# The first batch of a retention-and-Fourier kernel rebuilt: order of loads, sums on TensorE, an order of units written out by hand

## The chip, the core and the metric

One NeuronCore of a Trainium2 chip runs the kernel. The metric is the device time of one execution in microseconds; lower is better. A profile is one execution, recorded instruction by instruction; its span goes from the first to the last instruction, and the device time is a little longer than the span.

## What is computed

Inputs are q, k, v of shape (4 batches, 8 heads, 768 positions, 64), and two weights of 512 x 2048 and 2048 x 512. The first half is a linear recurrence with decay, the second a Fourier mixing and a feed-forward net:

```python
for t in range(S):                                    # S = 768
    state = gamma * state + k[:, :, t] (x) v[:, :, t] # outer product, per batch and head
    y[:, :, t] = scale * q[:, :, t] @ state
x = y as (batch, 768, 512)
X = fft(fft(x, axis=1), axis=2)
u = x + real(X)
un = (u - mean(u)) / sqrt(var(u) + 1e-6)              # over the 512 columns
out = u + relu(un @ w_ch1) @ w_ch2
```

## The kernel before

**The recurrence** is done in six chunks of 128 positions, two heads (a pair) at a time, four pairs per batch. q and k of a pair are cast to f16 (`q0_unit`, `k0_unit`; k is scaled by its decay, giving `kd`), transposed on TensorE (`t0_unit`, tile `tq`) and copied out of PSUM (`te_unit`: `qT`, `kT`). Scores inside a chunk (`am_unit`, tile `wkA`) are masked on VectorE (`ae_unit`, tile `atm`, four instructions per pair). Products of k and v per chunk (`kv0_unit`, tile `wkK`) go through a scan over the chunks (`sc_unit`, tile `s`). The output of a pair collects both parts in PSUM (`yi_unit`: masked scores times v; `yx_unit`: q times the states, tile `wkY`) and is scaled into `x` (`x0_unit`).

**The Fourier part** is two products with cosine and sine tables. Rows 0 to 383 and 384 to 767 of x are added and subtracted (`fold_s`, tile `xab`), then the two sides of the model axis (`fold_d`, tile `eo`), all on VectorE. Four products with the tables over the positions follow (`s1_unit`, tile `ps`, cast to `g`), then products with the tables over the model axis (`s2_unit`, tile `pq`), whose two halves are combined on VectorE, with ScalarE's copy `qn`, into `u`. The tables themselves are computed in the kernel: angles on VectorE (`trig_dve`), sines on ScalarE (`t_act`, `csn_unit`). In the first batch the first three blocks of 128 rows take a shorter way: `px_unit` puts x into PSUM by matmuls with half-identity matrices, and the mean comes from sums over x (`xmean_unit`).

**The feed-forward part** transposes `un` (`unT_unit`) and runs 16 blocks of the first product (`h0_unit` for the first half of batch 0, 128 rows at a time, tile `psh`; `h_unit` elsewhere), evicted with a relu by ScalarE or VectorE as `ACT_ROWS` says, and the second product (`ch_unit`, tile `psc`), whose result is scaled, added to u and stored.

**Order.** Batch 0's first part runs alone: `first_units` lists its units by hand, and `pin` makes every engine keep that order. `filler` matmuls with a zero operand stand in between. Everything behind is emitted from streams that have a start and an end in turns (`DM0`, `TS0`, `DA0`, `LD0` and so on), and is merged by those numbers: the feed-forward part of one batch beside the recurrence and the Fourier part of the next.

**Transfers.** Twelve loads of 384 KB bring batch 0: nine on SP's queue (L185), v of pairs 1 to 3 on ScalarE's queue. Eight DMAs of 512 KB bring the weights, cast to f16 on the way, issued by GpSimd (`w1_unit`, `w2_unit`) among its casts. The loads of batch 1 (L165) wait for the seventh weight DMA and for the last matmul of the second 128 rows of `h0_unit`:

```python
for x in (w_dma[after].ins, lb[0]["mm"].ins):         # after = 6
    tc.add_manual_dep(dma.ins, x.name, ...)
```

Of the kernel before, what the change touches and what calls it, by code (L numbers as in the profile page):

```python
# [18 lines left out]
P = 128  # L19
# [10 lines left out]
PAIR_ORDER = [0, 1, 3, 2]  # L30
ON_ACT = {'q': (0, 1, 0), 'kv': (1, 1, 1), 'g': (0, 1, 1), 'gr': (0, 0, 0)}
FB = 1
DM0, DM1 = (0.120, 0.208, 0.265, 0.344), (0.004, 0.137, 0.232, 0.341)
TS0 = (0.249, 0.368, 0.406, 0.410, 0.479, 0.544, 0.680, 0.685)
TS1 = (-0.040, -0.020, 0.048, 0.585)
DA0, DA1 = (0.068, 0.080, 0.173, 0.203, 0.315, 0.321), (0.063, 0.067, 0.063, 0.158, 0.168, 0.189)
LD0, LD1 = (0.172, 0.226), (-0.370, 0.140)
HT0 = (0.655, 0.675, 0.673, 0.628)
NPE = 2
ACT_ROWS = ((2, 5, 6, 7, 8, 9, 10, 14), (0, 3, 6, 7, 9, 10, 11, 12, 14, 15), (2, 4, 5, 6, 7, 8, 10, 14))  # L40
# [3 lines left out]
def kernel(  # L44
# [42 lines left out]
    cd16 = const.tile([P, 2, 257], f16, tag="cd16", padded_shape=[P, 2, 260])  # L87
    sd16 = const.tile([P, 2, 257], f16, tag="sd16", padded_shape=[P, 2, 260])
# [5 lines left out]
    gk5 = const.tile([P, NHP, D, NCH - 1], f32, tag="gk5")  # L94
# [85 lines left out]
    def first_load(name, i, eng):  # L180
        def run():
            h0 = 2 * PAIR_ORDER[i]
            t = in_of[name, 0, i] = inp.tile([P, 2, NCH, D], f32, tag="in32", name=f"{name}32")
            rows = "h (p c) d -> p h c d" if name == "q" else "h (c p) d -> p h c d"
            eng.dma_start(t, srcs[name][0, h0:h0 + 2].rearrange(rows, p=P))  # L185
        return run

    for i in range(4):
        for name in "qkv":
            if name != "v" or i == 0:  # L190
                first_load(name, i, nc.sync)()
# [34 lines left out]
    first_load("v", 1, nc.scalar)()  # L226
# [13 lines left out]
    def gk_unit(hp):  # L240
        def run():
            nc.scalar.copy(gk5[:, hp, :, 1:], gk2[:, hp:hp + 1].unsqueeze(1).to_broadcast(
                [P, D, NCH - 2]))
        return run
# [36 lines left out]
    def parity_consts():  # L281
        nc.vector.tensor_scalar(out=m2, in0=icol[:, 0:1], scalar1=0.5, scalar2=-0.25,
                                op0=ALU.mult, op1=ALU.add)
        nc.vector.tensor_scalar(out=m2, in0=m2, scalar1=MAGIC, scalar2=-MAGIC,
                                op0=ALU.add, op1=ALU.add)
        nc.vector.scalar_tensor_tensor(out=odd, in0=m2, scalar=-2.0, in1=icol[:, 0:1],
                                       op0=ALU.mult, op1=ALU.add)
        nc.vector.tensor_copy(pmask[:, 1:4:2], odd.to_broadcast([P, 2]))
        nc.vector.tensor_scalar(out=pmask[:, 0:4:2], in0=pmask[:, 1:4:2], scalar1=-1.0,
                                scalar2=1.0, op0=ALU.mult, op1=ALU.add)  # L290
        nc.vector.tensor_scalar(out=sgn, in0=odd, scalar1=-2.0, scalar2=1.0,
                                op0=ALU.mult, op1=ALU.add)

    def trig_dve(idx, n, w, col, coln):
        r = rs[2 * idx][:, 0:w]
        ra = rs[2 * idx + 1][:, 0:w]

        def run():
            nc.vector.tensor_scalar(out=ra, in0=kf[:, 0:w], scalar1=coln, scalar2=MAGIC,
                                    op0=ALU.mult, op1=ALU.add)  # L300
            nc.vector.tensor_scalar(out=ra, in0=ra, scalar1=-MAGIC, scalar2=float(n),
                                    op0=ALU.add, op1=ALU.mult)
            nc.vector.scalar_tensor_tensor(out=r, in0=kf[:, 0:w], scalar=col, in1=ra,
                                           op0=ALU.mult, op1=ALU.subtract)
        return run

    def ts_dve(c):
        return trig_dve(c, S, KN, icol[:, c:c + 1], icoln[:, c:c + 1])

    def csn_unit(c):  # L310
        def run():
            nc.scalar.activation(csn[:, c, :], rs[2 * c + 1][:, 0:384], AF.Sin, bias=hpi,
                                 scale=-float(2.0 * np.pi / S))
        return run

    def td_dve(c):
        return trig_dve(3 + c, DM, 257, icol[:, 3 + c:4 + c], icoln[:, 3 + c:4 + c])

    def t_act(idx, part):
# [5 lines left out]
        def run():  # L325
            if part == 0:
                nc.scalar.activation(ra, r, AF.Abs, bias=0.0, scale=1.0)
            elif idx < 3:
                src = (ra, r)[part - 1].rearrange("p (i t) -> p t i", t=2)
                dst = (csp, ssp)[part - 1]  # L330
                nc.scalar.activation(dst[:, :, idx, :], src, AF.Sin,
                                     bias=hpi if part == 1 else 0.0,
                                     scale=-sc if part == 1 else sc)
            else:
                src, dst = (ra, r)[part - 1], (cd16, sd16)[part - 1]
                nc.scalar.activation(dst[:, idx - 3, :], src, AF.Sin,
# [16 lines left out]
    hid, nhid = xts[1][:, 0, 0, 0:P], xts[1][:, 0, 1, 0:P]  # L353

# [5 lines left out]

    def half_ids():
        nc.gpsimd.tensor_scalar(out=hid, in0=ident16, scalar1=0.5, scalar2=1.0, op0=ALU.mult,
                                op1=ALU.mult)
        nc.gpsimd.tensor_scalar(out=nhid, in0=ident16, scalar1=-0.5, scalar2=1.0, op0=ALU.mult,
                                op1=ALU.mult)
# [47 lines left out]
    def k0_unit(i):  # L413
        def run():
            h0 = 2 * PAIR_ORDER[i]
            k32 = in_of.pop(("k", 0, i))
            kd = kd_of[0, i] = kp.tile([P, NCH, 2, D], f16, tag="kd16", name="kd16")
            nc.gpsimd.tensor_scalar(out=kd[:, :, 0, :], in0=k32[:, 0], scalar1=gkd[:, h0:h0 + 1],
                                    scalar2=1.0, op0=ALU.mult, op1=ALU.mult)
            if i < 3:  # L420
                nc.gpsimd.tensor_scalar(out=kd[:, :, 1, :], in0=k32[:, 1],
                                        scalar1=gkd[:, h0 + 1:h0 + 2], scalar2=1.0,
                                        op0=ALU.mult, op1=ALU.mult)
            else:
                nc.scalar.activation(kd[:, :, 1, :], k32[:, 1], AF.Copy, bias=0.0,
                                     scale=gkd[:, h0 + 1:h0 + 2])
        return run

    def v0_unit(i):
        def run():  # L430
            v32 = in_of.pop(("v", 0, i)).rearrange("p h c d -> p c h d")
            v16 = v16_of[0, i] = vp.tile([P, NCH, 2, D], f16, tag="v16", name="v16")
            n = NCH if i < 3 else 3
            last_cast[0, i] = nc.gpsimd.tensor_scalar(
                out=v16[:, 0:n], in0=v32[:, 0:n], scalar1=1.0, scalar2=1.0, op0=ALU.mult,
                op1=ALU.mult)
            if n < NCH:
                nc.vector.tensor_copy(v16[:, n:], v32[:, n:])
# [14 lines left out]
    def te_unit(i, part):  # L453
        def run():
            st = at[0, i]
            tq = st["tq", part]
            if part == 0:
                nc.scalar.copy(st["qT"].rearrange("p c t -> p (c t)").rearrange(
                    "p (t c) -> p t c", c=NCH), tq.rearrange("p c t -> p t c"))
            else:  # L460
                nc.scalar.copy(st["kT"], tq)
# [17 lines left out]
    def ae_unit(i, half, h2):  # L479
        def run():  # L480
# [3 lines left out]
                scalar=float(gam[2 * PAIR_ORDER[i] + h2] ** (-P)),  # L484
# [16 lines left out]
    def sc_unit(i):  # L501
        def run():
# [5 lines left out]
                data0=gk5[:, PAIR_ORDER[i]].rearrange("p e c -> p (e c)"),  # L508
# [3 lines left out]
    def yi_unit(i, h2):  # L512
        def run():
            st = at[0, i]
            first = i < 3
            if first:
                st["y", h2] = ps_y.tile([P, NCH, D], f32, tag="y", name="wkY",
                                        padded_shape=[P, 8, D])
            y, atm, v16 = st["y", h2], st["atm"], v16_of[0, i]
            for c in range(NCH):  # L520
                nc.tensor.matmul(y[:, c, :], atm[:, c, h2, :], v16[:, c, h2, :],
                                 start=first and c == 0, stop=not first and c == NCH - 1,
                                 skip_group_check=True)
        return run

    def yx_unit(i):
        def run():
            st = at[0, i]
            first = i == 3
# [663 lines left out]
```

## Time and profile before

| | us |
|---|---|
| median of 3 runs | 249.33 |
| lowest and highest | 247.75, 250.26 |
| span of the profiled execution | 246.5 |

Busy time of the engines and the span in 40 slices of 6.2 us (each digit is the busy share in tenths):

```profile
PE 233.7 (95%) x2024; PEld 144.1 (58%) x2024; DVE 177.0 (72%) x430; ACT 123.8 (50%) x276; POOL 81.0 (33%) x146
...
PE   6498899999999998999999999999999999999995
...
DVE  8689976897797878997886738897895657424112
ACT  2998769577775444662247424741248317202500
POOL 6657700465610047791000555670002305000000
DMA  8999999599999567999999657786200241221012
```

PE is TensorE, PEld its weight loads, DVE VectorE, ACT ScalarE, POOL GpSimd, SP the engine that issues most DMAs; a q behind a name is that engine's queue of DMA issues. "idle before" names what an engine waited for last.

### The profile page before, as it was taken

How to read it: one execution, taken by the hardware profiler on the slowest of the kernel's cores; microseconds unless marked ns; L12 is line 12 of the kernel's file. 1: busy time of each engine (PE TensorE's matmuls, PEld its weight loads, DVE VectorE, ACT ScalarE, POOL GpSimd, SP SyncE). 2: the span in 40 equal slices, each digit the busy share in tenths (PEclk: the TensorE clock that was granted, in tenths of full speed). 3: DMA queues.
4: the chain of work that ended last, by engine and by line, in shares of the span. 5: the costliest groups of instructions: out<-in, count | busy, mean ns of one | idle time of the engine just before them, and what ended most of it. 6: DMA issues, size and time to landing. Idle time of an engine off the chain costs nothing.

```text
span 246.5 us, 5306 instructions
## 1 busy us (share of the span) xinstructions
PE 233.7 (95%) x2024; PEld 144.1 (58%) x2024; DVE 177.0 (72%) x430; ACT 123.8 (50%) x276; POOL 81.0 (33%) x146
## 2 busy tenths in 40 slices
PE   6498899999999998999999999999999999999995
PEld 2165568956676655665567546565667455445543
DVE  8689976897797878997886738897895657424112
ACT  2998769577775444662247424741248317202500
POOL 6657700465610047791000555670002305000000
DMA  8999999599999567999999657786200241221012
GB/s 174 258 257 139 185 202 198 129 257 239 276 237 223 100 143 165 200 183 131 258 276 214 123 116 215 141 116 142 86 1 0 45 149 23 47 85 43 0 45 85
DMA packets 99209, 36.39 MB, mean 148 GB/s; under 512 B 89840, under 2 KB 96240, under 8 KB 99184
## 3 DMA queue, kind: packets, MB, share of 16 engines
q1 hardware_dynamic: 90304, 30.68, 58.9%
q0 software_dynamic: 4224, 4.19, 10.6%
q10 hardware_dynamic: 4656, 1.18, 2.9%
q8 instruction: 16, 0.26, 0.5%
q14 instruction: 9, 0.07, 0.1%
HBM read 27.26 MB, written 6.29 MB: 136 GB/s over the span
## 4 chain that ended last, share of the span: by engine, by line
PE 67%; DMA 10%; DVE 7%; ACT 5%; SPq 4%; POOL 4%; issue 2%; POOLq 0%; ACTq 0%; DVEq 0%
PE psc L990 30%; PE psh L947 24%; DMA k<-in_k_dram 8%; SPq L185 4%; PE ps L747 3%; PE wkA L611 3%; DMA q<-in_q_dram 2%; PE wkY L665 2%; PE wkY L661 1%; POOL u L881 1%; PE pq L844 1%; DVE bst L900 1%; POOL u L883 1%; DVE u L851 1%; ACT un L896 1%
## 5 line engine op out<-in xcount | busy, mean ns | idle before, releaser
L990 PE MATMUL psc<-w,ht 128*128 128x512 f16 (+2 forms) x400 | 89.3, 370 | 0.0
L947 PE MATMUL psh<-unT,w 128*128 128x384 f16 x448 | 81.6, 326 | 0.4 <-ACT ht L951 0.2
L990 PEld LDWEIGHTS <-ht 128*128 128x128 f16 x400 | 37.6, 98 | 36.4 <-issue 0.2
L947 PEld LDWEIGHTS <-w 128*128 128x128 f16 x448 | 42.3, 98 | 24.7 <-issue 1.4
L951 ACT ACTIVATE ht<-psh 128x384 f16<-128x384 f32 x64 | 30.9, 490 | 41.6 <-PE psh L947 41.1
L881 POOL TENSOR_TENSOR u<-u,x 128x256 f32<-128x256 f32 x21 | 13.4, 636 | 100.2 <-DVE u L851 89.7
L994 DVE SCALAR_TENSOR_TENSOR ob<-psc,stats,u 128x512 f32<-128x512 f32 (+2 forms) x25 | 18.1, 726 | 26.1 <-PE psc L990 26.0
L953 DVE TENSOR_SCALAR ht<-psh 128x384 f16<-128x384 f32 x48 | 26.2, 549 | 7.7 <-PE psh L947 7.3
L614 DVE TENSOR_TENSOR atm<-wkA,maskp 128x512 f16<-128x512 f32 x36 | 23.8, 683 | 1.6 <-PE wkA L611 1.6
L902 ACT ACTIVATE un<-u,stats 128x512 f16<-128x512 f32 x21 | 15.2, 722 | 16.5 <-DVE stats L901 12.3
L900 DVE BATCH_NORM_STATS2 bst<-u 128x6 f32<-128x512 f32 x21 | 14.6, 695 | 7.8 <-POOL u L883 7.6
L640 DVE SCALAR_TENSOR_TENSOR s<-s,gk,wkK 128x128 f16<-128x128 f16 x48 | 16.4, 342 | 3.5 <-ACT s L636 2.5
L673 ACT ACTIVATE x<-wkY,gexp 128x384 f16<-128x384 f32 x24 | 12.8, 581 | 8.2 <-PE wkY L665 8.2
L394 POOL TENSOR_SCALAR kd<-k,gexp 128x384 f16<-128x384 f32 x24 | 13.9, 588 | 3.6 <-DMA k<-in_k_dram 3.6
L151 PE MATMUL wps<-ht 128*128 128x512 f16 x40 | 13.0, 429 | 2.2 <-POOL ht L212 2.2
L883 POOL TENSOR_TENSOR u<-u,x 128x256 f32<-128x256 f32 x21 | 13.3, 636 | 3.0 <-DVE stats L901 2.4
L611 PE MATMUL wkA<-qTz,kT 128*128 128x256 f16 x72 | 13.4, 272 | 0.1
L846 ACT COPY qn<-pq 128x128 f32<-128x128 f32 x18 | 4.9, 273 | 13.5 <-PE pq L844 13.5
L964 PE MATMUL psh<-unT,w 128*128 128x128 f16 x192 | 11.5, 219 | 0.1
L964 PEld LDWEIGHTS <-w 128*128 128x128 f16 x192 | 11.0, 98 | 0.7 <-issue 0.5
L851 DVE SCALAR_TENSOR_TENSOR u<-pq,g,qn 128x256 f32<-128x256 f32 x18 | 8.5, 473 | 3.3 <-PE psh L947 2.5
L399 POOL TENSOR_SCALAR v<-v 128x768 f16<-128x768 f32 x12 | 10.0, 832 | 1.4 <-DMA v<-in_v_dram 1.3
(164 smaller groups left out, 315.0 us busy)
## 6 DMA issues: line engine op xcount, KB each, us to landing
q<-in_q_dram SPq DMA_DIRECT2D x16, 384.0 KB, 6.3
k<-in_k_dram SPq DMA_DIRECT2D x16, 384.0 KB, 5.9
out_dram<-ob SPq DMA_DIRECT2D x23, 256.0 KB, 2.7
v<-in_v_dram SPq DMA_DIRECT2D x13, 384.0 KB, 5.8
w<-in_moe_w_ch_dram POOLq DMA_DIRECT2D x8, 512.0 KB, 11.0
v<-in_v_dram ACTq DMA_DIRECT2D x3, 384.0 KB, 9.7
unT<-un SPq DMA_TRANSPOSE x15, 2.4
out_dram<-ob SPq DMA_DIRECT2D x1, 192.0 KB, 1.9
```

Of the source, the lines that this page charges most:

```text
L611: mm = nc.tensor.matmul(wk[:, c2], st["kT"][:, c, :], st["qT"][:, :, c, :], start=True, stop=True)
L614: nc.vector.tensor_tensor(out=st["atm"][:, 2 * part:2 * part + 2], in0=wk, in1=maskp[:, PAIR_ORDER[i]].unsqueeze(1).to_broadcast([P, 2, 2, ...
L640: nc.vector.scalar_tensor_tensor(out=s16[:, c], in0=s16[:, c - 1], scalar=gk2[:, hp:hp + 1], in1=wk[:, c - c0], op0=ALU.mult, op1=ALU.add)
L881: nc.gpsimd.tensor_tensor(out=u[:, kb, 0:256], in0=u[:, kb, 0:256], in1=x[:, kb, 0, 1:257], op=ALU.add)
L883: nc.gpsimd.tensor_tensor(out=u[:, kb, 256:512], in0=u[:, kb, 256:512], in1=x[:, kb, 1, 257:1:-1], op=ALU.add)
L900: nc.vector.bn_stats(bst, u[:, kb, :])
L947: nc.tensor.matmul(psh, w116[:, cb, fb * P:(fb + 1) * P], unT[:, cb, rt * 384:(rt + 1) * 384], start=(cb == 0), stop=(cb == 3))
L951: nc.scalar.activation(ht16[:, fb, :], psh, AF.Relu, bias=0.0, scale=-1.0)
L953: nc.vector.tensor_scalar(out=ht16[:, fb, :], in0=psh, scalar1=-1.0, scalar2=0.0, op0=ALU.mult, op1=ALU.max)
L964: mm = nc.tensor.matmul(psh[:, f], w116[:, cb, fb * P:(fb + 1) * P], unT[:, cb, kb * P:(kb + 1) * P], start=(cb == 0), stop=(cb == 3))
L990: nc.tensor.matmul(psc[:, c0:c1], ht16[:, fb, rb3 * P:(rb3 + 1) * P], w216[:, fb, c0:c1], start=(fb == 0), stop=(fb == NFB - 1))
L994: nc.vector.scalar_tensor_tensor(out=ob[:, c0:c1], in0=psc[:, c0:c1], scalar=lb[b]["st"][:, rb, 3:4], in1=lb[b]["u"][:, rb, c0:c1], op0=AL ...
```

## The change

Nothing is left out of the computation. In batch 0's first part:

- All twelve loads go on SP's queue, in a new order of pairs and with v of the last two pairs at the end.
- `first_units` becomes a string of unit names, `FIRST`, with the engine behind an @ where there is a choice (v VectorE, a ScalarE, g GpSimd). Casts of k and v, copies of the transposes, evictions of x and two table steps are split or moved by it.
- `fold_d` falls away: the sum over the two sides of the model axis is made by TensorE, which adds the products of both sides in PSUM (`s1b_unit`, with a negated sine table `ssn`). Each pair's columns of x are folded as soon as they are there (`fold_p`).
- The tables over the model axis are mirrored to 512 columns (`flip_unit`), so that a whole row of u stands in one PSUM tile; x is added by identity matmuls (`sa_unit`), and one instruction moves u out (`ua_unit`). The first block's centered rows are taken straight from PSUM (`n0_unit`); the others use the statistics.
- The position table `csn` is copied from the other tables on GpSimd, not computed by ScalarE.

Behind it the turns of the streams and `ACT_ROWS` take other numbers.

```diff
+ORD0 = [1, 0, 3, 2]
+LOADS0 = [("q", 0), ("k", 0), ("v", 0), ("q", 1), ("k", 1), ("v", 1), ("q", 2), ("k", 2),
+          ("q", 3), ("k", 3), ("v", 2), ("v", 3)]
+FIRST = """
+tsa2@g tsa0@v ts0 q0 ta00 ta01 ta02 xe1 k01@a k00@a ts2 tsa4@v fill6 t00 e00@a tsa3@g fill5 t01
...
+yi10 ta22 ae101 ae111 yi11 ta30 yx1 am20 gk2 k31@g fs0 s010 v21@g am21 t30 x11@v k30@a
+ae201 gk3 e30@a ae211 x10@v t31 e31@a ae210 fill4 am30 am31 ta41 w0 ae200 v32@g v22@v ae300 kv2
+sc2 s110 fl2@g yi21 yi20 ae310 ta31 fs1 yx2 v31@a x20@a w1 w2 s100 s000 ae311 ae301 kv3 yi31
+x21@a fs2 s001 sc3 s101 yi30 yx3 fl3@g x31@v ge00@a ge10@a x30@a fs3 gr2 xs0@a xs3@v csn w3
+sa00 sa10 sa11 g0 s011 s111 ge01@a xs1@v ge11@v gr0 sa20 sa02 sa01 sa03 g1 xs2@a mean sa22
+nh0@v g2 nh1@a sa12 pt0 gr3 sa13 ua0 sa21 pe0@a ua1 sa23 pt1 pe1@a gr1 bn1 ua2 w4 w5 w6 w7 bn2
+n1 n2
+"""
-DM0, DM1 = (0.120, 0.208, 0.265, 0.344), (0.004, 0.137, 0.232, 0.341)
-TS0 = (0.249, 0.368, 0.406, 0.410, 0.479, 0.544, 0.680, 0.685)
+DM0, DM1 = (0.101, 0.194, 0.248, 0.334), (-0.003, 0.131, 0.160, 0.383)
+TS0 = (0.282, 0.345, 0.387, 0.439, 0.487, 0.518, 0.675, 0.686)
...
-ACT_ROWS = ((2, 5, 6, 7, 8, 9, 10, 14), (0, 3, 6, 7, 9, 10, 11, 12, 14, 15), (2, 4, 5, 6, 7, 8, 10, 14))
+ACT_ROWS = ((5, 6, 7, 8, 9, 10, 13, 14), (0, 3, 6, 9, 12, 14, 15), (2, 4, 5, 7, 8, 10, 14))
...
-    for i in range(4):
-        for name in "qkv":
-            if name != "v" or i == 0:
-                first_load(name, i, nc.sync)()
+    for name, i in LOADS0:
+        first_load(name, i, nc.sync)()
...
+    def csn_unit():
+        for c in range(3):
+            nc.gpsimd.tensor_copy(csn[:, c].rearrange("p (i t) -> p t i", t=2),
+                                  csp[:, 0:2, c, 0:192])
...
+    def flip_unit(n, eng):
+        e = {"v": nc.vector, "g": nc.gpsimd}[eng]
+        out, in0, m = ((ssn, ssp, -1.0), (cd16[:, :, 257:512], cd16[:, :, 255:0:-1], 1.0),
+                       (sd16[:, :, 257:512], sd16[:, :, 255:0:-1], -1.0))[n - 2]
+
+        def run():
+            e.tensor_scalar(out=out, in0=in0, scalar1=m, scalar2=1.0, op0=ALU.mult,
+                            op1=ALU.mult)
+        return run
...
+    def fold_p(i):
...
+            lo, hi = {0: (1, 129), 2: (129, 258), 4: (130, 258), 6: (2, 130)}[h]
+            for a, op in ((0, ALU.add), (1, ALU.subtract)):
+                nc.vector.tensor_tensor(out=ab[:, a, :, side, lo:hi],
+                                        in0=x[:, 0:3, side, lo:hi],
+                                        in1=x[:, 3:6, side, lo:hi], op=op)
...
+    def s1b_unit(e, cb, side):
+        def run():
+            ab = fd[0]["ab"]
...
+            tab = csp if e == 0 else ssn if side else ssp
+            for par in range(2):
+                for sb in range(3):
+                    nc.tensor.matmul(ps[:, par, :], ab[:, par, sb, side, i0:i0 + 128],
+                                     tab[:, par, sb, :], start=(side == 0 and par == 0 and sb == 0),
+                                     stop=(side == 1 and par == 1 and sb == 2),
+                                     skip_group_check=True)
...
+    def sa_unit(kb, part):
+        def run():
...
+            ops = (((g[:, 0, sl], cd16[:, 0], 0, DM), (g[:, 2, sl], sd16[:, 0], 0, DM)),
+                   ((ident16, x[:, 0, 1:257], 0, 256), (ident16, x[:, 1, 257:1:-1], 256, DM)),
+                   ((g[:, 1, sl], cd16[:, 1], 0, DM),),
+                   ((g[:, 3, sl], sd16[:, 1], 0, DM),))[part]
+            for n, (lhsT, rhs, c0, c1) in enumerate(ops):
+                nc.tensor.matmul(pq[:, c0:c1], lhsT, rhs, start=(part == 0 and n == 0),
+                                 stop=part == 3, skip_group_check=True)
+        return run
+
+    def ua_unit(kb):
+        def run():
+            nc.vector.tensor_scalar(out=lb[0]["u"][:, kb], in0=lb[0]["pq", kb],
+                                    scalar1=fd[0]["g0"][:, kb:kb + 1], scalar2=0.0, op0=ALU.add,
+                                    op1=ALU.add)
+        return run
...
-        un += [yx_unit(3), yi_unit(3, 0), x0_unit(3, 0), filler(1), yi_unit(3, 1), x0_unit(3, 1),
-               g0_unit(0, (1,)), filler(1)]
-        un += [fold_s(0, 0, 130, 1, 2), fold_d(0, 0), s1_unit(0, 0, 0), fold_s(0, 130, 258, 1, 2),
-               px_unit(0), fold_d(0, 1, (0,)), xmean_unit(0), fold_d(0, 1, (1,)),
-               s1_unit(0, 1, 0), s1_unit(0, 0, 1), s1_unit(0, 1, 1), g0_unit(0, (2,)),
-               mean_unit(0)]
```

In the names of `FIRST`, ts and ta are table steps, q, k, v casts, t and e transposes and their copies, am and ae scores and masks, kv and sc the products and the scan, yi and yx the two parts of the output, x its eviction, fs and s folds and position products, ge casts of g, sa, ua, nh, n, bn, pt and pe the way of u to the transposed un, gk the decay row of the scan, fl the mirrors, w the weight DMAs, fill fillers.

## Prediction

> **What bounds the kernel now.** I read the busy time by stage first (columns: window, its length, busy time of TensorE, its weight loads, VectorE, ScalarE, GpSimd; granted clock, DMA share, GB/s):
>
> ```profile
> 24.00:36.20 12.20, 11.19 (x131) 7.22 (x130) 10.89 (x29) 8.13 (x21) 4.97 (x7) 1.00 1.19 194
> 42.00:50.00 8.00, 7.88 (x133) 7.54 (x132) 6.56 (x16) 4.99 (x12) 3.31 (x6) 1.00 0.73 152
> 50.00:64.00 14.00, 13.66 (x129) 8.59 (x128) 11.90 (x38) 11.28 (x19) 8.57 (x13) 1.00 1.20 256
> 64.00:80.00 16.00, 16.00 (x171) 10.99 (x169) 13.31 (x29) 10.88 (x21) 3.06 (x5) 1.00 1.15 237
> 90.00:100.00 10.00, 9.33 (x65) 5.26 (x64) 8.56 (x22) 4.03 (x9) 7.46 (x14) 1.00 0.90 193
> ```
>
> From 64 us on TensorE is full: its idle time there is 0.24 (80:90), 0.67 (90:100), 0.19 (150:160) and 0.37 (200:213), 1.5 us in all before the tail. What can be gained lies before 64 us, and only as far as the whole stream behind moves up. The chain of waits (the page's shares by line) agrees: feed-forward matmuls for more than half, then the DMA of k.
>
> ```profile
> PE 67%; DMA 10%; DVE 7%; ACT 5%; SPq 4%; POOL 4%; issue 2%; POOLq 0%; ACTq 0%; DVEq 0%
> PE psc L990 30%; PE psh L947 24%; DMA k<-in_k_dram 8%; SPq L185 4%; PE ps L747 3%; PE wkA L611 3%; DMA q<-in_q_dram 2%; PE wkY L665 2%; PE wkY L661 1%; POOL u L881 1%; PE pq L844 1%; DVE bst L900 1%; POOL u L883 1%; DVE u L851 1%; ACT un L896 1%
> ```
>
> Then the timeline of the first 64 us (start, duration, engine, line, work, in brackets the idle time before it and what ended it):
>
> ```profile
> 11.99 1.95 DVE L482 SCALAR_TENSOR_TENSOR atm<-wkA,maskf 128x384 f16<-128x384 f32 x4 [2.02 <-PE wkA L475]
> 23.71 2.29 POOL L1004 DMA_DIRECT2D w<-in_moe_w_ch_dram  x3
> 36.23 3.00 PE L964 MATMUL psh<-unT,w 128*128 128x128 f16 x48
> 42.23 4.63 PE L964 MATMUL psh<-unT,w 128*128 128x128 f16 x80
> 46.04 0.37 SPq L165 DMA_DIRECT2D q<-in_q_dram  x1
> 56.78 1.16 POOL L394 TENSOR_SCALAR kd<-k,gexp 128x384 f16<-128x384 f32 x2 [0.91 <-DMA k<-in_k_dram]
> 57.99 0.51 PE L567 MATMUL tq<-ident,kd 128*128 128x128 f16 x6 [0.23 <-POOL kd L394]
> 61.89 1.16 POOL L394 TENSOR_SCALAR kd<-k,gexp 128x384 f16<-128x384 f32 x2 [1.41 <-DMA k<-in_k_dram]
> ```
>
> The feed-forward starts at 36.23 (call it T). The loads of the second batch are issued at 46.04, and TensorE then runs just behind them: the transposes of kd at 57.99 and 63.10 start the moment GpSimd has cast a k that had just landed. So two chains must both move up: T, and the loads. The loads wait for the fourth of the five groups of 16 matmuls at 42.23 (42.23 + 0.8 x 4.63 = 45.9) and for the seventh weight DMA. Landing times of the weight DMAs issued at 23.7, 27.5 and 28.2 (last number: us to landing), and in the lines below them, last but one, the DMA share at the hand-over:
>
> ```profile
> w<-in_moe_w_ch_dram POOLq DMA_DIRECT2D x1, 512.0 KB, 5.5
> w<-in_moe_w_ch_dram POOLq DMA_DIRECT2D x1, 512.0 KB, 16.0
> w<-in_moe_w_ch_dram POOLq DMA_DIRECT2D x1, 512.0 KB, 17.8
> ...
> 44.00:45.00 1.00, 1.00 (x22) 1.00 (x20) 1.00 (x3) 0.18 (x1) 0.82 (x2) 1.00 0.55 90
> 45.00:46.00 1.00, 1.00 (x22) 1.00 (x20) 0.86 (x2) 0.60 (x1) 0.00 (x0) 1.00 0.18 33
> 46.00:47.00 1.00, 1.00 (x20) 0.98 (x18) 0.97 (x4) 0.63 (x1) 0.00 (x0) 1.00 0.00 0
> ```
>
> The second weight DMA lands at 29.2, the seventh at 43.5, the eighth at 46.0. The seventh is only 2.4 us off being what the loads wait for.
>
> **Loads.** All twelve loads of batch 0 now stand on SP's queue, v of the third and fourth pair last. The same twelve from SP alone are seen in batch 1: first issue 46.04, last v issued 61.13 and landed 6.5 later, 21.6 us. Before, with three on ScalarE's queue, the last landed at 12.02 + 10.9 = 22.9. So v3 lands at 22.4 to 22.9, v2 some 1.8 earlier. The last landing does not move; less work hangs on it. ScalarE's queue loses a stall of 3.69 us (its second table load waited for a load until 6.38).
>
> **VectorE, the pace of the first batch.** From its first mask (11.99) to its last fold (31.57) it had 19.6 us with little idle. New sum: 16 masks at 1.95 per four, 7.8; four scans at 0.81, 3.2; four evictions of x moved here, 0.49 each by the mask row (same shape from PSUM), 2.0; half a v cast 0.54; eight folds at 0.31, 2.5; one mirror of 510 elements, 0.3 to 0.6: 16.5. It can start earlier: with the table loaded by 4.0, ScalarE does abs 0.53, cosine 0.65, sine 0.55, the k halves at landing (6.05, two of 0.61), copies of qT 0.79 and kT 0.80: kT at 9.1 against 11.48. VectorE's own angle work, partly handed to GpSimd, lasts to about 10.1; that is the first mask. Added are waits for v2's landing, for the x of pair 2 and for pair 3's kv product behind two half DFTs on TensorE, 2.3 us: last fold at 28.9.
>
> **After the last fold.** Before, 4.66 us to T: a DFT half, cast, product, qn, u, un, transposes, copy. Now: two units of six matmuls (1.0), cast 0.60, last product 0.4, mean 0.3, centering 0.9 in two halves one behind the other, transposes and copy 0.9: 4.1. T = 33.0, gain 3.2. Behind it the last un must still precede the mask constants on ScalarE (1.69) and the eviction that frees TensorE's buffer; by VectorE's rows (three u at 0.68, two statistics at 0.86, small ones) that chain gains 2.7, and this is what the tensor chain offers.
>
> **TensorE's own work.** The DFT sums both sides on TensorE: 24 more matmuls of 193 columns at 0.087, +2.1; the u products 3.2 instead of 2.6; nine fillers fewer at 0.215, -1.9. +0.8 net, all ahead of T between waits; with no cover it would cost those 0.8.
>
> **GpSimd and the weights.** GpSimd takes six angle steps, four gk copies, two mirrors and three csn copies, and the weight DMAs stand behind some of them. The first comes after half of v2's cast and a gk copy: 20.44 becomes about 22.0. The second stands behind half of v3's cast (0.50, ends at 23.4) and the negated sine table, 1,158 elements; the rows 0.30 for 128 and 0.83 for 768 give 1.2, bounds 0.8 and 2.4: 23.71 becomes 24.6, bounds 24.2 and 25.8. From there the stream runs at the DMA's pace, 2.5 to 3.6 us a piece before; the fourth, issued at about 28.3, is still early enough. The seventh lands at 43.5 + 0.9 = 44.4. The Trainium skill ("DMA: Bandwidth & Descriptors", section on the anatomy of one DMA on the gpsimd path) fits 2.0 us plus bytes over 436 GB/s, which for 512 KB in a stream is 1.2 us a piece: the weights would be in by about 36 and could not hold the loads. The spacing of the landings is twice that, and the measurement decides.
>
> **The hand-over.** The fourth group of matmuls ends at about 43.4 now, so the weights take over as what the loads wait for: issue 44.4 instead of 46.04, 1.6 earlier. But the eighth weight DMA is still moving, where before the DMA stood idle from 45 to 47; that gives back about 0.5. The loads move up 1.1. The new order puts one more group of four output matmuls (0.86) ahead of pair 1's and pair 2's transposes, so less work is left behind the wait. Together 1.95, less than the 2.7 of the tensor chain, so this is the gain: 1.9.
>
> **Later turns.** 13 evictions move from ScalarE (0.490) to VectorE (0.549), 7.1 us in four batches. VectorE is 5.4 of 10 busy in 140:150 and 13.0 of 20 in 180:200, so they are covered; uncovered, each would hold TensorE as the two such waits of 0.2 do now. The shifted turns can close or reopen at most those 1.5 us; I take 0.
>
> Sum: 246.5 - 1.9 = 244.6 for the profiled execution. The median of the runs, 249.33, is 2.8 above the span: 247.4.
>
> **Rivals.**
> *The loads don't hold.* If k lands earlier than I think, the tensor chain decides: 2.7 to 3.2 plus part of the 1.5: about 246.2. For it: TensorE waited only 0.23 to 0.28 at these places. Against: it waited there at all.
> *Queues in a fixed order slip.* VectorE's x evictions and v2 cast, or ScalarE's k cast, hold what stands behind; T at 35.5 leaves 0.5 or less: 249.0. For it: 16.5 us of VectorE work leave no reserve.
> *Weights late (slower).* Every us of delay of the second weight DMA moves the loads one for one. The gain is gone at 1.95 + 0.9 = 2.9 us of delay, issue at 26.6. With the table flip and v3's landing both at their worst, and GpSimd stretched beside VectorE as VectorE's angle steps are now (257 elements took 0.30 and 1.01), issue at 27.6: 1 us slower, 250.3. Against: GpSimd's casts vary only 0.58 to 0.67.
> *Clock.* The first six fillers take 0.43 each, those at 7.73 0.21, so TensorE starts at half rate though the granted clock reads 1.00; it kept the full rate over an idle stretch of 2.98 us. If, with nine fillers fewer, it fell back before T, some 8 us of matmuls double and T comes 4 us later: 250.1. The Trainium skill ("TensorE: Matmul & The Clock Gate", Part 1) puts the fall at an idle window of about 3.4 us; none in the new order should be over 1.5.
>
> **Chances.** Forecast 0.52 (own range 246.3 to 248.7, from the bounds of the table flip and the hand-over); loads don't hold 0.22; slip 0.15; weights late 0.08; clock 0.03. Within 1% (2.5 us, about what a measurement can tell) lie the forecast but for a fifth of it, most of the slip and half of the slower ones; faster by more: 0.22 x 0.85 + 0.1 = 0.29; slower by more: 0.06. Range 245.0 to 250.2, from the tensor chain with a us of the later gaps to weights late.
>
> **What would show it.** Feed-forward's first group at 33 (32 to 34.5); SP's first load of batch 1 released by the weights at 44 to 45; kd transposes of pairs 1 and 2 at about 56.9 and 62, waiting for GpSimd longer than 0.3 us; GpSimd's second weight DMA at 24.2 to 25.8; the granted clock and the 0.215 of a 512-column matmul unchanged; the last 180 us alike. Wrong, if the first load is released by a matmul, or T is past 35.

## The result and the profile after

The median went from 249.41 us (247.75 to 250.8, 19 runs) to 247.66 us (246.9 to 249.17, 19 runs): ratio 0.993, 95% interval 0.9912 to 0.9949, a gain of 1.75 us. The forecast was 247.4. But the profiled execution does not show that gain: its span is 246.7 us, 0.2 longer than the one before. So the agreement of the median says little until it is known where the gain comes from.

The changed kernel first, by stage (columns as in the same table of before, and two later stages added):

```profile
24.00:36.20 12.20, 10.61 (x132) 7.37 (x131) 10.77 (x28) 4.99 (x13) 8.62 (x12) 1.00 1.12 174
42.00:50.00 8.00, 8.00 (x127) 7.17 (x124) 6.80 (x16) 4.87 (x10) 3.69 (x6) 1.00 1.17 227
50.00:64.00 14.00, 13.57 (x127) 8.33 (x126) 10.34 (x32) 10.70 (x17) 8.41 (x12) 1.00 1.16 246
64.00:80.00 16.00, 16.00 (x170) 10.92 (x169) 15.27 (x34) 9.65 (x19) 2.82 (x4) 1.00 1.16 245
90.00:100.00 10.00, 9.54 (x70) 5.65 (x68) 8.61 (x22) 4.84 (x12) 8.49 (x15) 1.00 0.93 160
140.00:150.00 10.00, 9.47 (x52) 4.61 (x50) 4.72 (x10) 2.08 (x5) 3.48 (x6) 1.00 0.72 138
160.00:180.00 20.00, 19.56 (x170) 11.51 (x169) 16.18 (x35) 6.04 (x14) 4.23 (x7) 1.00 0.57 107
```

TensorE is still full between 64 and 140 us but for 0.46, and now idles 0.53 between 140 and 150 and 0.44 between 160 and 180, where it was full before. The shares of the chain of waits moved away from TensorE, which had 67% before:

```profile
PE 59%; DVE 13%; DMA 9%; POOL 8%; SPq 4%; ACT 3%; issue 3%; POOLq 0%; ACTq 0%; DVEq 0%
```

VectorE went from 7% to 13% and GpSimd from 4% to 8%. Added up by stage from the pieces of the chain, VectorE's rise lies mostly ahead of 64 us (9.2 us of the chain before, 21.0 now). GpSimd's lies behind it, and is largest between 130 and 160 us (1.0 to 8.0), where TensorE also lost most (23.9 to 9.3): there the chain now runs through the wait at 147 us. The landmarks of the timeline, in the form of before:

```profile
10.67 0.55 DVE L514 SCALAR_TENSOR_TENSOR atm<-wkA,maskf 128x384 f16<-128x384 f32 x1
24.90 1.54 POOL L1114 DMA_DIRECT2D w<-in_moe_w_ch_dram  x2
35.16 2.73 PE L1074 MATMUL psh<-unT,w 128*128 128x128 f16 x46 [0.35 <-ACT unT L950]
45.37 0.37 SPq L181 DMA_DIRECT2D q<-in_q_dram  x1
57.41 0.50 PE L596 MATMUL tq<-ident,kd 128*128 128x128 f16 x6
62.77 0.51 PE L596 MATMUL tq<-ident,kd 128*128 128x128 f16 x6 [0.36 <-POOL kd L423]
```

The first mask came 1.3 earlier (11.99 to 10.67). The feed-forward runs through from 35.16 (two of its matmuls stand at 34.54), 1.07 earlier than 36.23; I call this time T, as in the prediction. The first load of batch 1 goes out at 45.37, 0.67 earlier. The transposes of pair 1 stand at 57.41 without a wait, those of pair 2 at 62.77 after 0.36. So the start did move, by about a third of what was forecast, and this one execution gave it back later, most of it behind 64 us. It is one of the slower executions: its time was 248.40, 0.7 above the median.

### The profile page after: what moved, and what is told of

Its sections match the earlier page's. It is cut to its first block, busy times and chain, and to the rows that moved or that the text cites. A ratio compares the mean times of both kernels' runs of the same rounds, so it can differ in the third digit from the quotient of the medians.

```text
span 246.7 us, 5319 instructions
## 1 busy us (share of the span) xinstructions
PE 234.6 (95%) x2033; PEld 144.5 (59%) x2033; DVE 184.3 (75%) x438; ACT 113.3 (46%) x248; POOL 86.4 (35%) x156
## 3 DMA queue, kind: packets, MB, share of 16 engines
HBM read 27.26 MB, written 6.29 MB: 136 GB/s over the span
## 4 chain that ended last, share of the span: by engine, by line
PE 59%; DVE 13%; DMA 9%; POOL 8%; SPq 4%; ACT 3%; issue 3%; POOLq 0%; ACTq 0%; DVEq 0%
PE psh L1057 23%; PE psc L1100 22%; DMA k<-in_k_dram 5%; SPq L201 3%; DVE bst L1019 3%; POOL u L1008 3%; PE wkA L640 3%; PE ps L823 3%; DMA unT<-un 2%; DMA kT<-kd 2%; POOL kd L423 2%; POOL u L1006 1%; PE wkY L694 1%; DVE atm L514 1%; DVE ht L1083 1%
## 5 line engine op out<-in xcount | busy, mean ns | idle before, releaser
L1061 ACT ACTIVATE ht<-psh 128x384 f16<-128x384 f32 x51 | 24.7, 489 | 45.2 <-PE psh L1057 45.0
L1063 DVE TENSOR_SCALAR ht<-psh 128x384 f16<-128x384 f32 x61 | 33.0, 550 | 8.6 <-PE psh L1057 8.0
L1021 ACT ACTIVATE un<-u,stats 128x512 f16<-128x512 f32 x21 | 15.2, 722 | 17.8 <-DVE stats L1020 14.2
L167 PE MATMUL wps<-ht 128*128 128x512 f16 x31 | 9.4, 447 | 2.1 <-POOL ht L226 2.1
L640 PEld LDWEIGHTS <-kT 128*128 128x128 f16 x72 | 6.8, 98 | 5.9 <-DMA kT<-kd 0.9
```

The source lines that it names most:

```text
L640: mm = nc.tensor.matmul(wk[:, c2], st["kT"][:, c, :], st["qT"][:, :, c, :], start=True, stop=True)
L1061: nc.scalar.activation(ht16[:, fb, :], psh, AF.Relu, bias=0.0, scale=-1.0)
L1063: nc.vector.tensor_scalar(out=ht16[:, fb, :], in0=psh, scalar1=-1.0, scalar2=0.0, op0=ALU.mult, op1=ALU.max)
```

## The experiments

There are three sets of runs, the first on one chip, the second and third on another. Each has runs of the kernel before beside it, with medians of 249.27, 249.83 and 249.75 us; ratios are to those. Each run lists the mean granted clock of its execution, and this turned out to matter.

**Before, profiled again.** The same code as before.

> The kernel before, a second profile. Reason: times of the kernel before lie 1.7 us above the span if they stand as those of the changed kernel do (248.4 beside 246.7), so its profiled span of 246.5 would be a time of 248.2, well below its median of 249.4. Theory A (that one execution was a lucky one, by waits of TensorE after 64 us): this span is 247 to 248.5, the first 64 us agree within 0.3 us (feed-forward at 36.2, first load of batch 1 at 46.0), and the extra 0.5 to 2 us are waits of TensorE after 64 us. Rival B (the executions differ already in the first batch): the feed-forward or the first load stands over 0.5 us from 36.2 and 46.0.

The span is 248.8 us, T is 38.62 and the first load goes out at 48.43: rival B. The windows of that execution (last but two: granted clock) the product behind TensorE's idle stretch, and T:

```profile
8.00:10.00 2.00, 0.61 (x3) 0.10 (x1) 1.93 (x3) 1.90 (x5) 1.60 (x2) 1.00 1.33 242
10.00:12.00 2.00, 0.43 (x10) 0.43 (x12) 0.04 (x1) 1.97 (x5) 1.15 (x2) 0.63 1.28 233
12.00:14.00 2.00, 2.00 (x24) 1.20 (x21) 1.81 (x4) 1.07 (x2) 1.54 (x4) 0.50 1.22 284
14.00:16.00 2.00, 2.00 (x10) 0.90 (x8) 1.86 (x8) 1.57 (x3) 1.21 (x3) 0.50 1.24 253
16.00:18.00 2.00, 2.00 (x31) 1.62 (x29) 0.06 (x2) 1.25 (x3) 0.56 (x1) 0.66 1.27 264
...
11.57 0.82 PE L475 MATMUL wkA<-qTz,kT 64*128 64x128 f16 x12 [2.96 <-ACT kT L461]
38.62 3.00 PE L964 MATMUL psh<-unT,w 128*128 128x128 f16 x48
```

The clock falls to 0.50 from about 10.5 to 17.4 us, 6.8 us: all of the two windows from 12 to 16, and by their means of 0.63 and 0.66 some three quarters of the one ahead of them and two thirds of the one behind. The product that took 0.51 in the first profile, behind 2.98 us of idle time, takes 0.82:

```profile
11.53 0.51 PE L475 MATMUL wkA<-qTz,kT 64*128 64x128 f16 x12 [2.98 <-ACT kT L461]
```

Over a span of 248 us a spell of 3.4 us at half rate lowers the mean by 0.007 and two by 0.014, and the 87 runs of the kernel before fall into just these groups: 13 at 0.998 to 1.00, 51 at 0.991 to 0.993, 23 at 0.986. On the first chip their medians are 247.97, 249.27 and 250.44: a spell costs the kernel before about 1.3 us, two cost 2.5. The profile from which I predicted is of the first kind: its clock is 1.000.

The changed kernel has 28 runs, 19 of the result and 9 of a later set. Of these 21 are at 0.998 to 1.00 (medians 247.55 and 247.81), 7 at 0.993 (247.91 and 248.22), none below. At clock 1.00 its 7 runs of the last set still spread from 247.37 to 248.37, where the 8 of the kernel before in the first set have 247.65 to 248.13: the changed kernel differs from run to run by something else as well.

**Closing the idle stretch of before by fillers.** In the list of units of the kernel before:

```diff
-k0_unit(0), t0_unit(0, 1), filler(3), te_unit(0, 1)
+k0_unit(0), t0_unit(0, 1), filler(14), te_unit(0, 1)    # and filler(9) in the second run
```

> The kernel before with 14 fillers instead of 3 behind the first k transposes, 11 more of 0.215 us, so that TensorE's idle stretch of 2.98 us (8.55 to 11.53) shrinks to about 0.6; nothing else is changed. The runs of the kernel before fall in three groups by granted clock: 1.00 (median 247.95), 0.993 (249.27), 0.986 (250.44); in the profile of the third the clock is 0.50 from 10.5 to 17.4, just behind that stretch. Theory A (the idle stretch makes the clock fall to half for one or two spells of 3.4 us, and most of the measured gain of the change is that it closes the stretch): nearly all runs at clock 1.00, median 247.8 to 248.1, 1.2 to 1.5 us faster than the kernel before. Rival B (the dips come by chance or by load): the three groups stay, median 249.0 to 249.5 or more. Rival C (11 more fillers delay the chain): clock 1.00 but a time over 248.5.

> The kernel before with 9 fillers instead of 3 behind the first k transposes, so that the idle stretch of 2.98 us shrinks to about 1.7 and the product behind it starts when it did (11.53). With 11 more it started 0.04 later, and four tiny VectorE operations then met GpSimd's casts (0.74, 0.55 and 0.53 instead of 0.16 to 0.17), T was 0.56 later. Theory A (the idle stretch makes the clock fall; the fillers themselves cost nothing): 10 or more of 12 runs at clock 1.00, median that of the kernel before's runs at 1.00 on the same chip, within 0.3 us, some 1.2 to 1.5 us under its median. Rival B (a stretch of 1.7 is enough for a fall): the three groups stay. Rival C (fillers cost by themselves): clock 1.00, but over 0.7 us above the 1.00 group of the kernel before.

With 11 more fillers all 12 runs had a clock of 1.00, but the median was 249.26 (ratio 0.9969, 0.9951 to 0.9988), 1.0 above the three runs of before at 1.00 in that set (248.25): theory A for the clock, rival C for the time. With 6 more, 9 of 12 runs had 1.00 and the median was 248.31 (0.9952, 0.9927 to 0.9977), 1.44 under the kernel before and equal to its two runs at 1.00 in that set (248.33): theory A, though it had asked for ten runs at 1.00. Its windows from 8 to 18 all read 1.00, with an idle stretch of 1.33 instead of 2.96:

```profile
11.70 0.51 PE L475 MATMUL wkA<-qTz,kT 64*128 64x128 f16 x12 [1.33 <-ACT kT L461]
```

So in the old first batch the stretch brings the falls: 74 of 87 runs have one with it, 3 of 12 with 6 fillers more, none of 12 with 11 more. Six matmuls on a zero operand bring 1.4 us there.

What the 11 fillers gave back is partly seen: the product behind them began 0.04 later, and three operations of VectorE that take 0.16 to 0.17 otherwise then ran beside GpSimd's casts. First VectorE's, then GpSimd's, of the run with 11:

```profile
14.98 0.74 DVE L286 SCALAR_TENSOR_TENSOR odd<-m,icol 128x1 f32<-128x1 f32 x1
15.75 0.55 DVE L288 COPY pmask<-odd 128x2 f32<-128x2 f32 x1
16.33 0.53 DVE L289 TENSOR_SCALAR pmask<-pmask 128x2 f32<-128x2 f32 x1
...
14.88 0.83 POOL L409 TENSOR_SCALAR q16z<-q 128x768 f16<-128x768 f32 x1
15.69 0.59 POOL L418 TENSOR_SCALAR kd<-k,gexp 128x384 f16<-128x384 f32 x1
16.25 0.59 POOL L421 TENSOR_SCALAR kd<-k,gexp 128x384 f16<-128x384 f32 x1
```

Add start and duration: they end at 15.72, 16.30 and 16.86, GpSimd's three at 15.71, 16.28 and 16.84. Each of these operations on one or two elements per partition ends when GpSimd's instruction does. T was 36.79, 0.56 late. The run with 6 more fillers has the same three at 0.61, 0.55 and 0.53 and the same T in its profile, though, and its median is low, so why the 11 cost 0.9 more than the 6 stays open.

**The changed kernel without its fillers.** All six `fill` entries are taken out of `FIRST` (25 matmuls); the six ahead of it stay.

> The changed kernel without the 25 fillers of its first batch (the six ahead of it stay): TensorE idles in stretches of 1 to 2.5 us up to 12 us. Theory A (idle stretches make the clock fall): most runs below 1.00, at 0.993 or 0.986; each spell at half clock cost the changed kernel only about 0.4 us where it fell at 15.0 to 18.4, but 1.3 where it falls at 10 to 17 as before; median 248.2 to 250. Rival B (the dips come from load, and fillers add to it): the clock is 1.00 in more runs than the 14 of 19 of the changed kernel, median 247.4 to 247.7.

Median 248.01 (0.9929, 0.9904 to 0.9954), not clearly slower than with them (0.993 and 0.9916). Eight runs read 1.00, one 0.993, three 0.979, and those three took 247.36 to 248.03. Theory A had most runs below 1.00; that failed. Rival B failed too: 8 of 12 at 1.00 are not more than 14 of 19, and the median lies above its 247.7. The profile shows why the column can't be read alone here. Six transposes, early and late (both windows read 1.00):

```profile
16.66 0.82 PE L481 MATMUL tq<-ident,q16z 128*128 128x128 f16 x6
20.53 0.49 PE L481 MATMUL tq<-ident,q16z 128*128 128x128 f16 x6
```

TensorE ran at half rate until about 18 us, without a fall being recorded, and yet T was 35.92, only 0.76 later than with the fillers. The old first batch lost 2.4 us of T to 6.8 us at half rate. In this one profile half rate up to 18 us cost the new first batch 0.76.

**When the loads of batch 1 may start.** `load_unit(1, i, 6)` becomes 7, and in another run 5.

> The changed kernel with the loads of the second batch waiting for the eighth weight DMA (landed at 47.8) instead of the seventh (45.3). First load at 47.8 instead of 45.4, 2.4 later. Theory A (loads and tensor chain are about even: TensorE waited 0 at pair 1 and 0.36 at pair 2 for a cast k): nearly all of it comes through, the kernel takes 1.6 to 2.4 us longer than the changed one, 249.3 to 250.0. Rival B (the loads have slack): under 0.8 us longer, under 248.5.

> The changed kernel with the loads of the second batch waiting for the sixth weight DMA instead of the seventh. The matmul that they also wait for ends at 44.7, so the first load moves from 45.4 to 44.7. Theory A (the tensor chain now decides, the loads only by the 0.36 us of wait at pair 2): 0.2 to 0.4 us faster than the changed kernel, 247.3 to 247.5. Rival B (the loads decide): 0.65 us faster, 247.0. Rival C (loads that run beside the last two weight DMAs land no earlier): no change.

The first load of batch 1, with the eighth and with the sixth weight DMA:

```profile
47.25 0.37 SPq L181 DMA_DIRECT2D q<-in_q_dram  x1
44.66 0.37 SPq L181 DMA_DIRECT2D q<-in_q_dram  x1
```

With the eighth it goes out at 47.25 and the median is 249.59 (1.002, 0.9993 to 1.0047), 1.9 above the changed kernel: theory A, the loads have no slack, and the price in the rival "weights late", one for one, is right. With the sixth it goes out at 44.66 and the wait of 0.36 at pair 2 is gone, but the median is 247.61: no change, rival C in its number. Its mechanism is out: GpSimd cast the k of pairs 1 and 2 at 55.00 and 60.42, where the changed kernel had 55.99 and 61.56, so the loads do land earlier. In the profile of this run T is 34.96, and its timeline shows no wait of TensorE of 0.2 between 41 and 90 us and none at 147; it is the fastest of its 12 executions (246.84).

**GpSimd beside VectorE's folds.** In `FIRST` the negated sine table (`fl2`) moves ahead of the second half cast of v, `csn` behind `x21`, and its copies go to ScalarE; in a second run also `load_unit(1, i, 5)`:

```diff
-... fs0 s010 v21@g ... sc2 s110 fl2@g yi21 ... x21@a fs2 ... xs3@v csn w3
+... fs0 s010 fl2@g v21@g ... sc2 s110 yi21 ... x21@a csn fs2 ... xs3@v w3
-            nc.gpsimd.tensor_copy(csn[:, c]...
+            nc.scalar.copy(csn[:, c]...
```

> The changed kernel with the negated sine table made earlier on GpSimd (in its idle time at 19.0 to 21.5) and the three csn copies on ScalarE (idle from 25.6 to 28.5), so that no table work of GpSimd stands beside VectorE's folds. In the changed kernel the four folds beside it took 1.22, 0.72, 0.60 and 0.71 us, the four others 0.35 to 0.37. Theory A (GpSimd's work stretches them, and they set the feed-forward's start): all eight take 0.35 to 0.40, the last fold ends at 29.3 instead of 31.0, the feed-forward runs from 33.6 instead of 35.2; the second weight DMA is issued at 23.8 instead of 24.9, the loads at 44.5 instead of 45.4; 0.8 to 1.4 us faster than the changed kernel, 246.3 to 246.9. Rival B (the folds are long for another reason): they stay over 0.6 and the feed-forward stays at 35. Rival C (another wait takes the place: TensorE's half DFTs or ScalarE's copies): folds short, but gain under 0.3 us.

> Both edits together: GpSimd's table work away from VectorE's folds, and the loads of the second batch waiting for the sixth weight DMA. Theory A (T is now set by the chain that VectorE and TensorE share, the folds are a part of it): with no fall of the clock T is 34.4 to 34.8 and the loads are issued at 44.1 to 44.5; 0.3 to 0.7 us faster than the changed kernel of the same call. Rival B (what the folds gave is waited for elsewhere, as in the run with the folds alone, where VectorE waited 1.07 twice for TensorE): T at 35, within 0.3 us of the changed kernel.

In the changed kernel a fold, what GpSimd did beside it, and a fold with no table work beside it; then, in the run with both edits, the first of these folds with the one behind it (two in 0.63), and T:

```profile
24.01 1.22 DVE L736 TENSOR_TENSOR xab<-x 128x384 f16<-128x384 f16 x1
23.79 1.17 POOL L352 TENSOR_SCALAR ssn<-ssp 128x1158 f16<-128x1158 f16 x1
30.36 0.36 DVE L736 TENSOR_TENSOR xab<-x 128x384 f16<-128x384 f16 x1
...
23.97 0.63 DVE L736 TENSOR_TENSOR xab<-x 128x384 f16<-128x384 f16 x2
33.71 2.73 PE L1074 MATMUL psh<-unT,w 128*128 128x128 f16 x46 [0.35 <-ACT unT L950]
```

The long fold ends 0.27 after GpSimd's instruction (24.96), about as if it had begun then. The second fold of that pair (25.15, 0.72) stood beside the issue of a weight DMA and no table; other folds beside such issues took 0.35 and 0.36, so its length is not explained. With both edits all eight folds take 0.35 to 0.43 (sum 2.6 instead of 4.4, overlaps left out), and T is 33.71 instead of 35.16: theory A holds for T, beyond its range, and rival B for the time. With the folds alone one fold still took 0.78, beside the mirror of the cosine table, and the clock fell in the profiled execution (0.50 for 3.4 us from 15.2); T was 35.25, against 35.76 in the run with the later gate, whose clock fell at the same place. If the gate has no part in T, that fall cost the kernel with the folds 1.54 us of T (35.25 to 33.71), more than the 0.76 above.

The median does not follow. The folds alone: 248.13 (0.9962, 0.9935 to 0.9989), not faster than the changed kernel, the number of rival C, though the fall hides what T would have been. Both edits: 247.78 (0.9904, 0.9868 to 0.9939), beside 247.82 (0.9916) of the changed kernel in the same set. TensorE's waits behind T in the run with both edits:

```profile
50.19 0.40 PE L1044 MATMUL pst<-ident,un 128*128 128x128 f16 x4 [0.23 <-ACT un L1021]
61.48 0.51 PE L596 MATMUL tq<-ident,kd 128*128 128x128 f16 x6 [0.39 <-POOL kd L423]
108.15 1.02 PE L1100 MATMUL psc<-w,ht 128*128 128x512 f16 x4 [0.55 <-ACT ht L1061]
146.95 1.46 PE L1057 MATMUL psh<-unT,w 128*128 128x384 f16 x8 [0.78 <-DVE ob L1104]
```

The second is the loads again, though they go out at 43.42. The first three, 1.17 us of the 1.4 gained, are waits that the changed kernel's second profile (next run) does not have; the last it has. But this execution (248.24) is the slowest of its seven. Three of the others took 246.65 to 247.05, less than any of the changed kernel's nine in this set (247.37 and up), so the gain at T comes through in some executions and not in others. In both runs with the folds the device time also lies 2.05 above the span in the median, against 1.78 in the changed kernel's; where those 0.27 us go is not shown.

**The changed kernel again.**

> The changed kernel once more, on one chip with the runs below and with a second profile. In eight profiles so far the span less the start of the feed-forward (T) is 210.1 to 210.5, but 211.4 in two that waited about a us at 140 to 166 us, and 211.9 where the loads were held. Theory A (T carries the gain; what stands behind it is alike): most runs at clock 1.00, T at 34.9 to 35.7, span less T 210.1 to 211.5; ratio to the kernel before 0.991 to 0.995. Rival B (the gain comes from behind T): T over 36.

Median 247.82, ratio 0.9916 (0.9887 to 0.9945); T 35.12, span 246.2. Span less T is 210.2 to 210.5 in the five profiles with the old first batch, 211.5 and 211.1 in the two of the changed kernel, whose wait at 147 us (0.53 and 0.79) makes a good part of the difference; three variants of the changed kernel had 210.1 to 210.3, and the other four, which waited there or for held loads, 210.8 to 212.5. All signs of theory A are met: T moves the end, but about 1 us of what it brought was lost behind it in these two executions.

**The turns alone, and the first batch alone.** The constants `DM0` to `HT0` and `ACT_ROWS` are exchanged between the two kernels.

> The changed kernel with the turn constants and the list of ScalarE's evictions of before, the new first batch alone. At clock 1.00 the changed kernel's median is 247.55, the one of before 247.95, though the feed-forward started 1.07 us earlier; in the profile TensorE lost 0.53 at 147 us and 0.44 at 165.7, which the profile of before doesn't have. Theory A (the shifted turns give it back): without them these two waits are gone, 246.9 to 247.2 at clock 1.00. Rival B (the waits come with the earlier stream itself, by its loads and transposing DMAs, whatever the constants): they stay in some place, 247.4 to 247.8. Rival C (the new constants are worth something, the output matmuls put ahead of the transposes above all): 248 or more, with TensorE waiting over 0.5 us at the transposes of pairs 1 and 2.

> The kernel before with the new turn constants and the new list of ScalarE's evictions, the old first batch. Theory A of the run with the old constants (the shifted turns give back): 0.3 to 0.8 us slower than the kernel before at equal clock, 248.3 to 248.8 at clock 1.00. Rival B (no effect of their own): 247.8 to 248.1. Rival C (worth something): 247.0 to 247.6, with no wait at the transposes of pair 1 (0.23 before).

The new first batch with the old constants: 247.91 (0.9928, 0.9903 to 0.9954). The old first batch with the new constants: 249.99 (1.0017, 0.999 to 1.0043). At clock 1.00 the first has 247.92 (8 runs), the second 248.94 (3 runs, against 248.25). The first batch makes the whole gain; the shifted turns bring nothing that can be measured. In the old first batch they cost 0.7 at clock 1.00, as theory A has it, but on three runs each; in the new one taking them back gained nothing. The waits at 147 us are gone with the old constants, and 0.20 and 0.33 at the transposes of pairs 1 and 2 and 0.67 at 95 us come in their place.

**v in the pairs' turn.** In `LOADS0`, `("v", 2)` goes ahead of `("q", 3)`.

> The changed kernel with v of the third pair loaded ahead of q and k of the fourth, as the pairs' turn would have it, instead of behind them. q and k of the fourth pair land one load, about 1.8 us, later; GpSimd waited 0.64 and 0.68 us for them already, so its casts come some 1.8 later, and with them the transposes at 19.7 and 20.2, and the last masks. Theory A (VectorE's chain has no reserve): T 0.8 to 1.8 later, 0.8 to 1.8 us slower than the changed kernel of the same call. Rival B (the fourth pair has slack, since VectorE works through the third meanwhile): under 0.4 us.

Median 249.38 (0.998, 0.9958 to 1.0002), 1.56 above the changed kernel of the same set, and 1.35 at clock 1.00 (249.16 to 247.81): theory A. TensorE now waits for the casts of q and k of the fourth pair:

```profile
20.71 0.51 PE L481 MATMUL tq<-ident,q16z 128*128 128x128 f16 x6 [0.94 <-POOL q16z L438]
22.19 0.82 PE L481 MATMUL tq<-ident,kd 128*128 128x128 f16 x6 [0.97 <-POOL kd L452]
```

In eight of 12 runs the clock fell; in the profile it did so from 21.5 to 25.0 us, behind these waits, and T was 37.05. With the new order of the units, v loaded last is worth most of what the change brings: without it the changed kernel at clock 1.00 (249.16, 4 runs) is slower than the kernel before (248.33, 2 runs).

## Why the prediction was right in its number and mostly wrong in its reason

The forecast of 247.4 came near 247.66 by luck. The span, which it built on, was to fall by 1.9 us and rose by 0.2 in the profile; most of the gain of the median comes from a cost of the kernel before that the sum does not have. By its own sign ("wrong, if T is past 35") it failed: T was 35.16 and 35.12 in two profiles, though the first two matmuls stood at 34.54 and 34.49.

*What bounds.* "TensorE is full from 64 us on, the gain must come from before" held: the new first batch alone makes the gain. "The last 180 us alike" did not hold, since waits of 0.53 and 0.44 came in behind 140 us.

*The sum's last step was the wrong one.* "The median is 2.8 above the span" took the profiled execution for a typical one. The runs list both numbers, and time less span lies about 1.8 (1.7 to 2.1). The other 1.0 is what the spells at half clock cost the median: 74 of the 87 runs of before have them and the profiled one had not. I wrote that TensorE "kept the full rate over an idle stretch of 2.98 us" and counted the clock as a risk of the change, at 0.03; it was a cost of the kernel before, at that very stretch. In the last set six fillers in the old batch bring 1.44 of the 1.93 us that the change brings (medians 249.75, 248.31, 247.82). The rest, 0.5, is also what runs at clock 1.00 show (248.33 to 247.81, only two runs of before), and is not clear of noise: the two ratios' intervals overlap. The Trainium skill ("TensorE: Matmul & The Clock Gate", Part 1) has a free-running window of 3413 ns; spells of 3.4 and 6.8 us agree. By its rule of thumb ("HAM oscillation") only idle gaps over about 3.4 us matter; here, with a stretch of 2.98 and 2.96 in the two profiles, 74 of 87 runs have a fall, and the runs decide.

*VectorE's sum, 16.5 us and T = 33.0.* The terms were right but for two. The first mask came at 10.67, not 10.1. Eight folds "at 0.31, 2.5" took 4.4, because all were priced as if alone and two of the four pairs ran beside GpSimd's tables; the run with the negated sine and `csn` away from them got T to 33.7. In all VectorE was busy 17.98 us from its first mask to its last fold (30.99), not 16.5, and idle 2.34, as forecast (2.3). What follows the last fold was forecast as 4.1 and took 4.2 (30.99 to 35.16). So in the profile the tensor chain gained 1.07, not 2.7 to 3.2. TensorE's own work grew by 0.9 of busy time (0.8 forecast) and cost nothing that shows.

*Weights and hand-over.* "The weights take over as what the loads wait for" was right. The second weight DMA was issued at 24.90 (24.6 forecast) but landed at 32.0, 7.1 later instead of 5.5; the seventh landed at 45.2 instead of 44.4, and the first load went out with it at 45.37. The 1.2 us a piece that the prediction set aside counts the 512 KB of f16 that a weight DMA writes; the f32 bytes that it reads are twice that (the page has 27.26 MB read from HBM, and 2 x 512 x 2048 x 4 bytes, 8.39 MB, of them are weights). Who released it, by SP's waits:

```profile
SPq L181 <- DMA w<-in_moe_w_ch_dram: 27.9, 1, 27.9
```

No wait for a matmul stands in that answer any more. The loads moved up 0.67, not 1.6.

*The gain of 1.9* was to show at the transposes of pairs 1 and 2. Four output matmuls fewer are left behind them (368 and not 372 of tile `psc` at pair 1, 356 and not 360 at pair 2), which is 0.86. So the lead was 57.99 - 57.41 + 0.86 = 1.44 at pair 1 and 63.10 - 62.77 + 0.86 = 1.19 at pair 2. The span still came out 0.2 longer, so 1.4 to 1.6 was lost behind in this profile, where "later turns" were taken at 0 with 1.5 either way; that the turns themselves lost it is not shown.

*Rivals.* "Queues slip, T at 35.5" is what the profile came nearest to, though by stretched folds and not by a slipped queue. "Loads don't hold" is out: 1.9 us later loads cost 1.9 us. "Clock", at 0.03, named the right thing at the wrong kernel.

## What to carry to other kernels

Before a time is added to a profile, look at the granted clock of several runs: one profile shows one execution, and a mean of 0.993 instead of 1.00 was 1.3 us for the kernel before and 0.4 for the changed one. An idle stretch of TensorE near 3 us is worth closing with matmuls on zeros even where the chain does not wait for them; try several numbers of them, since 6 brought 1.4 us here and 11 only 0.6. A gain at the head of a stream that is full behind is not kept for certain: 1.4 us more at T left the median where it was, and in the execution that was profiled waits at 50, 61 and 108 us took 1.17 of it.

## What the runs showed of the hardware

Not expected: some VectorE operations whose inputs lie in SBUF ended only with the GpSimd instruction beside them, down to 128x1 operations of 0.16 us that took 0.74, and a fold of 0.36 that took 1.22; masks, which read their scores from PSUM, took 0.53 to 0.54 beside GpSimd's tables. The Trainium skill ("SBUF — State Buffer", section on the two separate sides) describes a port pair of both engines that one instruction holds to its end; the common ends above agree.

Also not expected: the granted clock reads 1.00 for a TensorE that has not yet reached full rate (until 18 us without fillers), and three runs at 0.979 were not slower than others. A long idle stretch is also not the only thing that a fall comes behind: in the run with v in the pairs' turn it fell at 21.5 us behind stretches of 0.94 and 0.97, and in the run with the later gate at 15.0 behind none over 0.5 since TensorE began. Why the three runs at 0.979 cost nothing, why the clock still fell in 3 of 12 runs with an idle stretch of 1.33, and what sets the waits at 147 us, stays open.
